# Fifteen constant matmuls into an unread PSUM tile ahead of each attention layer

## The chip, the cores and the metric

The kernel runs on one core of one Trainium2 chip. The metric is the device time of one execution in microseconds, the median over several runs. The core has a matmul engine (TensorE, in the profile PE, its weight loads PEld), a vector engine (VectorE, DVE), an activation engine (ScalarE, ACT), GpSimd (POOL) and a queue for transfers (SyncE, SP). Matmuls write to PSUM, which has eight banks; the other engines copy the results from there to SBUF.

## The reference

Four layers run one after the other on an array `x` of 2048 positions by 512 channels: convolution, attention, convolution, attention. Each adds its result to `x`, and each works on a layer norm of `x`. The two convolutions share their parameters, and so do the two attention layers.

```python
x = A_u
x = x + _A_ref(_layernorm(x), ...)            # long convolution, as a product of spectra
x = x + _B_ref(_layernorm(x), B_wqkv, B_wo)   # attention over 8 positions, 2 apart
x = x + _A_ref(_layernorm(x), ...)
x = x + _B_ref(_layernorm(x), B_wqkv, B_wo)

def _B_ref(x, wqkv, wo):                      # H = 32 heads of 16, W = 8, dil = 2
    q, k, v = split(x @ wqkv)
    logits = einsum("bhsd,bhswd->bhsw", q, k[pos - 2*w]) * 16 ** -0.5   # w = 0..7, masked before 0
    o = einsum("bhsw,bhswd->bhsd", softmax(logits), v[pos - 2*w])
    return o.reshape(B, S, D) @ wo
```

## The kernel before, in words

`x` stays in SBUF as a tile `X` of 128 partitions by 16 groups `j` by 512 channels. `kernel_and_first_conv` builds the convolution's kernel and does the first convolution; `b_layer` does an attention layer; `a_layer` does the second convolution; `b_layer` is then called again. In what follows, the first place is the passage from the first convolution to the first attention layer, and the second place is the passage from the second convolution to the second attention layer.

Inside a layer the order of the work on each engine is fixed: the layer records its operations in a `Plan`, and `Plan.run` issues them in the order of a written list of numbers. What an engine has in its queue is done in that order. Semaphores hold an instruction until its operands are ready and until the PSUM or SBUF buffer that it writes has been read by its last user. PSUM pools are opened per layer, so the first tile of a pool in `b_layer` lies in banks that the convolution before it used.

A convolution ends with the matmuls into `ps_y` (L849 and L852 in the first one, L1089 and L1092 in the second), which ScalarE copies back to `X` (L856 and L1097).

An attention layer begins with its layer norm. For each of four groups of four `j`, VectorE gathers the statistics of `X` (L150, L159), ScalarE takes the root (L163), VectorE inverts it and makes the offset (L175, L187), and the two engines write the normed rows `xn` (VectorE at L190, ScalarE at L1154). Two of the eight pairs of rows are transposed by TensorE, eight 128x128 matmuls each, into `pt_x` (L1165), and copied to `xnT` by ScalarE (L1168). The other six pairs are transposed by transfers (L1160). From `xnT` TensorE makes the values `ps_v` (L1210, eight matmuls of 256 columns for a pair) and the queries and keys `ps_qk` (L1190, four matmuls of 512 columns for each block), which ScalarE and VectorE copy to `VX`, `qT` and `kT` (L1215, L1195). `ps_v` and `ps_qk` take turns in a pool `psA` of two PSUM banks. VectorE then multiplies `qT` with shifted `kT` into `prod` (L1241), TensorE sums these into `Lp` (L1251), and after the softmax VectorE multiplies the weights with shifted `VX` (L1353), TensorE sums over `w` (L1369, L1374) and multiplies with `wo` (L1426).

`ident` is the 128x128 identity and `C["F1T"]` a constant table of the convolution; both are loaded once at the start and stay in SBUF.

Of the kernel before, what the change touches and what calls it, by code (L numbers as in the profile page):

```python
# [13 lines left out]
F32 = mybir.dt.float32  # L14
# [1104 lines left out]
def b_layer(nc, tc, C, X, Wt, VX, ln_b, part, evac, done, VSTAT_Q):  # L1119

    with ExitStack() as es:
# [8 lines left out]
        psA = es.enter_context(tc.tile_pool(name="b_psA", bufs=2, space=PSUM))  # L1130
        ident, bones = C["ident"], C["bones"]
# [3 lines left out]
        kT = [qk.tile([128, 2, NK * 128 + S], BF, name=f"kT{fp}") for fp in range(2)]  # L1135
        qT = [qk.tile([128, 2, S], BF, name=f"qT{fp}") for fp in range(2)]
        L = [sm.tile([128, NJ, 2, W, 8], BF, name=f"L{fp}") for fp in range(2)]
        box = {}
        pl = Plan(psA=2, psL=1, psO=2, prod=4, LT=3, sm1=1, sm2=1, sm_m=1, sm_s=1, rdb=1)
        turned, Kd, Qd, Kx, Vd, Ld, Sd, Od = {}, {}, {}, {}, {}, {}, {}, {}  # L1140
# [88 lines left out]
        def logits(fp, jh, halves):  # L1229
# [46 lines left out]
            def evac():  # L1276
                nc.scalar.copy(L[fp][:, j0:j0 + 8].rearrange("p j t (q w) h -> p q (j t) (w h)", q=2),
                               box.pop(("l", fp, jh))[:].rearrange("p q b j (t x) -> p q (b j t) x", t=2))
# [11 lines left out]
        def softmax(fp, j0, j1):  # L1290
            n = j1 - j0
            Lf = L[fp][:, j0:j1].rearrange("p j t w h -> p (j t) w h")

# [19 lines left out]
            def mask():  # L1313
                for w in range(1, W):
                    k = min(j1, DIL * w)
                    if k > j0:
                        nc.gpsimd.memset(L[fp][0:1, j0:k, :, w, :], -1e9)

# [26 lines left out]
        def pv(fp, j0, nj):  # L1345
            flat, np = fp == 0 or j0 < 12, min(nj, 4)

            def part(w, first):
                a = j0 - DIL * w

                def prod():
# [3 lines left out]
                        VX[:, fp, NV + a:NV + a + nj].rearrange("p j (t d h) -> p (j t) d h", t=2, d=DH),  # L1355
                        L[fp][:, j0:j0 + nj, :, w, :].rearrange("p j t h -> p (j t) h").unsqueeze(2)
                        .to_broadcast([128, nj * 2, DH, 8]), ALU.mult)
# [120 lines left out]
def kernel(  # L1478
# [36 lines left out]
    with tc.manual_schedule():  # L1515
        with tc.tile_pool(name="mid", bufs=1) as mid:
# [40 lines left out]
            def stored(pl, q, after):  # L1557
                pl.op("S", 2.0, lambda: nc.sync.dma_start(ov[:, q * 4:q * 4 + 4, :], X[:, q * 4:q * 4 + 4, :]), *after, lag=2.7)
            b_layer(nc, tc, C, X, Wt, VX, ln_b, 2, summed, normed, BN_Q)
            a_layer(nc, tc, C, X, kt_dram, U, ln_b2)  # L1560
        b_layer(nc, tc, C, X, Wt, VX, ln_b2, 1, lambda j, ps: nc.scalar.copy(X[:, j, :], ps), stored, range(4))


# [28 lines left out]
```

## Time and profile before

| | |
|---|---|
| median of 6 runs | 530.82 us (530.10 to 531.24) |
| the profiled execution's own time | 530.8 us |
| its span, first to last instruction | 528.9 us |
| mean granted TensorE clock | 0.962 |
| PE busy | 406.0 us, 77% of the span |
| DVE busy | 475.5 us, 90% |
| ACT busy | 339.3 us, 64% |

Busy time is the time in which an engine has at least one instruction running; matmuls overlap, so a busy PE is not PE at its peak. The granted clock is a record of its own: 1.00 is full speed, 0.50 half. In a table by windows, each row is a stretch of the span in us from its start, with each engine's busy time and count of instructions, the granted clock and the transfers. In the chain of work that ended last, each row has its start, its length and what ran.

### The profile page before, as it was taken

To read this page: it belongs to the slowest core of one execution; us is meant where nothing else is said; L and a number is where in the kernel's file an instruction comes from. 1 tells how busy PE (TensorE), PEld (TensorE's weight loads), DVE (VectorE), ACT (ScalarE), POOL (GpSimd) and SP (SyncE) were. 2 spreads that over 40 slices of the span, in tenths; PEclk is the share of its full clock that TensorE was granted. 3 is DMA by queue.
4 is the path that set the end of the run, shared out by engine and by line. 5 is a ranking of instruction groups with operands and counts; after the bars stand their busy time and mean duration, and the time that the engine had idled before them with its cause. 6 is when DMAs were issued, how large, how long until landed. Compare 5 with 4: busy or idle time off the path is not lost.

```text
span 528.9 us, 11869 instructions
## 1 busy us (share of the span) xinstructions
PE 406.0 (77%) x4943; PEld 239.5 (45%) x4943; DVE 475.5 (90%) x803; ACT 339.3 (64%) x505; POOL 12.9 (2%) x62
## 2 busy tenths in 40 slices
PE   0202367689868769689999779969994999997896
PEld 0100244456655547443356334555773433652352
DVE  4999999999999999749899998889989497999995
ACT  3999956886856758662666137989996436641230
POOL 0000000000000003000000000000000000000000
PEclk9999997989988989979999999999997999998998
DMA  8300074248135253460011522679401500232242
GB/s 265 152 1 0 0 141 93 59 127 149 43 122 102 61 142 101 144 120 31 0 56 46 100 50 40 152 234 174 81 2 20 101 30 32 71 50 60 40 131 89
DMA packets 88922, 45.08 MB, mean 85 GB/s; under 512 B 74923, under 2 KB 81068, under 8 KB 88612
## 3 DMA queue, kind: packets, MB, share of 16 engines
q1 hardware_dynamic: 87284, 43.93, 34.7%
q8 instruction: 38, 0.62, 0.5%
q10 hardware_dynamic: 1584, 0.39, 0.4%
q14 instruction: 16, 0.13, 0.1%
HBM read 15.77 MB, written 8.13 MB: 45 GB/s over the span
## 4 chain that ended last, share of the span: by engine, by line
PE 37%; DVE 31%; ACT 10%; issue 8%; DMA 3%; POOL 0%; SPq 0%; DVEq 0%; ACTq 0%
PE ps_qk L1190 11%; DVE prod L1353 6%; PE ps_v L1210 4%; PE Lp L1251 3%; DVE Ttab L488 3%; DVE Ttab L481 3%; DVE ln_st_b L150 2%; DVE Y2tab L545 2%; DVE Ttab L545 2%; DVE Ttab L480 2%; PE po L1369 2%; PE ps_o L1426 2%; PE po L1374 1%; ACT X L598 1%; DVE prod L1241 1%
## 5 line engine op out<-in xcount | busy, mean ns | idle before, releaser
L1241 DVE TENSOR_TENSOR prod<-qT,kT 128x2048 bf16<-128x2048 bf16 (+1 forms) x80 | 77.1, 1004 | 15.0 <-ACT kT L1195 14.3
L1353 DVE TENSOR_TENSOR prod<-VX,L 128x2048 bf16<-128x2048 bf16 (+2 forms) x96 | 77.5, 861 | 1.9 <-PE po L1374 0.9
L1190 PE MATMUL ps_qk<-xnT,wqk 128*128 128x512 bf16 x256 | 63.1, 385 | 0.1
L1369 PE MATMUL po<-prod,sb_ident 128*128 128x512 bf16 x224 | 56.0, 386 | 7.3 <-DVE prod L1353 4.9
L1369 PEld LDWEIGHTS <-sb_ident 128*128 128x128 bf16 x224 | 21.7, 99 | 35.8 <-issue 12.3
L1190 PEld LDWEIGHTS <-wqk 128*128 128x128 bf16 x256 | 22.6, 99 | 31.6 <-issue 10.8
L1210 PE MATMUL ps_v<-wv,xnT 128*128 128x256 bf16 x256 | 34.4, 281 | 0.8 <-ACT xnT L1168 0.6
L1389 ACT CAST ot<-po 128x1024 bf16<-128x1024 f32 x14 | 13.6, 1014 | 30.0 <-PE po L1369 30.0
L1251 PE MATMUL Lp<-prod,sb_bones 128*32 128x512 bf16 x256 | 28.6, 388 | 4.2 <-DVE prod L1241 4.2
L520 PE MATMUL ps_sum<-Ttab,sb_ident 128*128 128x512 bf16 x18 | 7.8, 433 | 30.4 <-DVE Ttab L480 27.6
L716 ACT CAST Z<-ps_s 128x1024 bf16<-128x1024 f32 (+1 forms) x32 | 29.3, 988 | 0.8 <-PE ps_s L711 0.4
L1215 ACT CAST VX<-ps_v 128x512 bf16<-128x512 f32 x32 | 18.8, 587 | 17.0 <-PE ps_v L1210 17.0
L558 PE MATMUL psk<-Ttab 128*32 128x64 bf16 x1024 | 21.8, 205 | 9.6 <-DVE Ttab L545 6.1
L545 DVE TENSOR_TENSOR Ttab<-Ttab,MPA 128x2048 bf16<-128x2048 bf16 (+2 forms) x20 | 28.4, 1433 | 0.3
L1210 PEld LDWEIGHTS <-xnT 128*128 128x128 bf16 x256 | 23.9, 100 | 9.8 <-issue 4.6
L1426 PE MATMUL ps_o<-wo_t,oT 128*128 128x512 bf16 x112 | 28.0, 379 | 0.0
L561 PE MATMUL psk<-Y2tab,Ttab 128*32 128x48 bf16 x1024 | 21.9, 200 | 7.1 <-issue 7.1
L545 DVE TENSOR_TENSOR Y2tab<-Ttab,MPB 128x6144 bf16<-128x6144 bf16 (+1 forms) x13 | 27.2, 2118 | 0.0
L150 DVE BATCH_NORM_STATS2 ln_st_b<-X 128x6 f32<-128x128 bf16 (+2 forms) x80 | 23.0, 357 | 3.7 <-ACT X L856 3.3
L1195 ACT CAST kT<-ps_qk 128x512 bf16<-128x512 f32 x26 | 15.2, 584 | 16.8 <-PE ps_qk L1190 16.8
L1195 ACT CAST qT<-ps_qk 128x512 bf16<-128x512 f32 x24 | 14.0, 584 | 18.5 <-PE ps_qk L1190 18.5
L558 PEld LDWEIGHTS <-Ttab 128*32 128x32 bf16 x1024 | 19.8, 103 | 12.2 <-issue 11.5
(218 smaller groups left out, 1024.8 us busy)
## 6 DMA issues: line engine op xcount, KB each, us to landing
X<-in_A_u_dram SPq DMA_DIRECT2D x8, 512.0 KB, 5.3
kt_scratch<-sp_k SPq DMA_DIRECT2D x16, 256.0 KB, 3.1
Kt<-kt_scratch SPq DMA_DIRECT2D x16, 256.0 KB, 6.1
out_dram<-X SPq DMA_DIRECT2D x4, 512.0 KB, 2.7
k_scratch<-KTq SPq DMA_DIRECT2D x7, 256.0 KB, 2.7
KT<-k_scratch SPq DMA_DIRECT2D x7, 256.0 KB, 3.0
VX<-VX SPq DMA_DIRECT2D x4, 448.0 KB, 3.8
kT<-kT SPq DMA_DIRECT2D x8, 192.0 KB, 2.2
```

The source lines that it names most:

```text
L150: self.nc.vector.bn_stats(self.st[:, j, part, :], X[:, j, a:b])
L545: nc.vector.tensor_tensor(d, src.to_broadcast([128, c, n, 2 * EYB]), mm.to_broadcast([128, c * n, EYB, 2]), ALU.mult)
L558: nc.tensor.matmul(o.rearrange("e (s i) -> e s i", s=2), xs, T[:, 1:3, h, m // 2, :, t], start=(m == 0), stop=False, skip_group_check=True)
L716: nc.scalar.copy(box["Z", kind, dc][:, 0:n // 8, :, jq * 32:(jq + 1) * 32].rearrange("p g r k -> p r g k"), box.pop(("s1", kind, dc, jq))[ ...
L1190: nc.tensor.matmul(ps[:], wqk[:, ct, f0:f0 + 128], xnT[:, 4 * s:4 * s + 4, ct, :], start=(ct == 0), stop=(ct == 3))
L1195: copy((qT, kT)[which][fp][:, f2, o:o + 512], box.pop(("qk", which, fp, f2, s))[:])
L1210: nc.tensor.matmul(ps[:, jj].rearrange("p t h d -> p (t h d)"), xnT[:, j + jj, ct, :], wv[:, ct, fp * 256:(fp + 1) * 256], start=(ct == 0) ...
L1241: nc.vector.tensor_tensor(pr[:, 0:n2], qT[fp][:, a:a + n2, j0 * 128:j0 * 128 + 1024], kT[fp][:, a:a + n2, c0:c0 + 1024], ALU.mult)
L1251: nc.tensor.matmul(Lp[r0:r0 + 32, w // 4, :], bones[:, w % 4, :], pr[:, f2 - a, hb * 512:(hb + 1) * 512], start=(n == 1), stop=(n == 4), s ...
L1353: nc.vector.tensor_tensor(p2[:, 0:nj].rearrange("p j t d h -> p (j t) d h"), VX[:, fp, NV + a:NV + a + nj].rearrange("p j (t d h) -> p (j ...
L1369: nc.tensor.matmul(po[:, c:c + 512], ident[:], p2[:, k + j:k + j + 2].rearrange("p j t d h -> p (j t d h)"), start=(n == 1), stop=(n == W))
L1426: nc.tensor.matmul(ps, box["oT"][:, ft // 2, j, ft % 2, :], wo_t[:, ft, :], start=(ft == 0 and not res), stop=(ft == 3))
```

## The change

Right after `b_layer` has made its tiles and before it records its plan, it takes a tile `idle` of one PSUM bank from `psA` and issues fifteen matmuls of 128 rows by 512 columns into it. The weights are `ident`, the moving operand is the first two groups of `F1T`. Each starts and ends its own sum, so each overwrites the one before. Nothing reads the tile. As `b_layer` is called twice, thirty matmuls and thirty loads of `ident` are added in all.

```diff
         L = [sm.tile([128, NJ, 2, W, 8], BF, name=f"L{fp}") for fp in range(2)]
+        idle = psA.tile([128, 512], F32, name="idle", tag="psA")
+        for _ in range(15):
+            nc.tensor.matmul(idle[:], ident[:], C["F1T"][:, 0:2].rearrange("p j r k -> p (j r k)"), start=True, stop=True)
         box = {}
         pl = Plan(psA=2, psL=1, psO=2, prod=4, LT=3, sm1=1, sm2=1, sm_m=1, sm_s=1, rdb=1)
```

In TensorE's queue the fifteen stand behind the last `ps_y` matmul of the convolution and ahead of the first `pt_x` transpose. The first of them waits for ScalarE: for the copy of the last `ps_y` tile to `X`. The first user of `psA` in the plan, a `ps_v`, moves from the pool's first bank to its second, and all later users move along with it. The queues of the other engines are the same as before.

## The prediction

> **What bounds the kernel now.** The page gives two limits that take turns:
>
> ```profile
> PE 406.0 (77%) x4943; PEld 239.5 (45%) x4943; DVE 475.5 (90%) x803; ACT 339.3 (64%) x505; POOL 12.9 (2%) x62
> ...
> PE 37%; DVE 31%; ACT 10%; issue 8%; DMA 3%; POOL 0%; SPq 0%; DVEq 0%; ACTq 0%
> ```
>
> The first line is busy time, the second the shares of the chain that ended last. PE leads the chain although DVE is busier, so there are stages in which PE alone sets the end. The chain in order of time shows one of them at the first place:
>
> ```profile
> 225.59 0.82 ACT xn L1154
> 226.41 0.05 issue
> 226.46 1.05 PE pt_x L1165 x8
> ...
> 227.58 1.02 ACT xnT L1168
> 228.60 0.05 issue
> 228.65 1.89 PE ps_v L1210 x8
> 230.54 8.71 PE ps_qk L1190 x36
> ```
>
> and at the second:
>
> ```profile
> 406.26 1.05 PE pt_x L1165 x8
> ...
> 408.45 1.69 PE ps_v L1210 x8
> 410.14 7.77 PE ps_qk L1190 x36
> ```
>
> The same 36 matmuls take 8.71 us at one place and 7.77 at the other, and the 8 into `ps_v` 1.89 and 1.69, where later in the layer the chain has them at 0.98. What differs is the clock. I then asked for windows of 3.41 us, the step in which the clock record changes in this trace:
>
> ```profile
> 222.08:225.50 3.42, 0.00 (x0) 0.00 (x0) 3.42 (x29) 1.22 (x4) 0.00 (x0) 1.00 0.00 0
> 225.50:228.91 3.41, 2.15 (x18) 1.82 (x19) 3.41 (x13) 2.92 (x5) 0.00 (x0) 0.50 0.13 25
> 228.91:232.32 3.41, 3.41 (x13) 1.74 (x12) 1.23 (x4) 1.22 (x3) 0.00 (x0) 0.50 1.05 192
> 232.32:235.74 3.42, 3.42 (x17) 1.57 (x16) 0.00 (x0) 2.30 (x4) 0.00 (x0) 1.00 1.12 189
> 399.58:402.99 3.41, 0.52 (x9) 0.35 (x7) 3.41 (x17) 1.37 (x3) 0.00 (x0) 1.00 0.00 0
> 402.99:406.40 3.41, 0.14 (x2) 0.15 (x3) 3.41 (x28) 2.19 (x5) 0.00 (x0) 0.50 0.00 0
> 406.40:409.82 3.42, 3.11 (x23) 2.48 (x22) 3.42 (x14) 1.93 (x2) 0.00 (x0) 0.50 0.40 75
> ...
> 146.99:150.40 3.41, 1.44 (x12) 0.82 (x12) 3.41 (x6) 3.41 (x4) 0.00 (x0) 1.00 0.53 196
> 177.71:181.12 3.41, 1.46 (x173) 1.34 (x159) 3.41 (x7) 2.31 (x3) 0.00 (x0) 1.00 0.13 27
> ...
> 474.67:478.08 3.41, 1.39 (x12) 0.58 (x8) 3.19 (x4) 0.55 (x2) 0.00 (x0) 1.00 1.12 128
> ```
>
> The first figure after the length is PE busy, the third from the end the granted clock. A window in which PE rested (0.00 and 0.52 us) is followed by windows at half clock. At the first place the clock is half from 225.50 to 232.32, at the second from 402.99 to 409.82. PE restarts at 226.46 and 406.26, so 5.86 us and 3.56 us of half clock fall on work. The last three rows place the border: 1.44 us (42%) and 1.39 us (41%) closed the clock for the next window, 1.46 us (43%) did not. For opening, the window with 2.15 us (63%) at 225.50 did not do it, the one with 3.11 us (91%) at 406.40 did. The rest comes from layer norm: PE's two waits for `xn` are 4.74 and 6.15 us.
>
> **Does earlier PE work move the end?** At the first place DVE has nothing to do from 230.14 to 238.18 but wait for `kT`, which comes from the `ps_qk` blocks. From 240 to 325 it is over 90% busy in nearly every stretch. So DVE starts earlier by what PE wins, and the rest of the layer with it. The transfers could spoil this: six transposes by transfer are issued from 227.26 to 234.10 and land at most 4.0 us later, so by 238.1 at the latest. The block that reads the last of them starts at 241.66, and 2.3 us earlier is 239.4, still behind the landing. The blocks that read the first two start at about 235.2, or 232.9 with the gain, against landings by 228.63 + 4.0 = 232.6. This cover is thin (0.3 us); typical landings at 3.4 us leave 0.9.
>
> **The burst itself.** A 512-column matmul at full clock takes its turn every 0.216 us (7.77 / 36), and the loads of `ident` hide under it: the chain has 8 of the `po` matmuls, which also load `ident` each time, in 1.73 us, 0.216 each. Fifteen take 3.24 us. At the first place they wait for the last copy L856, which ends at 221.92 + 0.57 = 222.49; the burst issues from about 222.55 to 225.79 and the first transpose wants PE at 226.46, so 0.67 us are spare. At the second place the last copy L1097 ends at about 400.73, the burst goes from 400.8 to 404.0, and 2.2 us are spare. The windows before both bursts are 76% and over 90% busy, so both start at full clock. The burst is therefore free as long as one matmul takes under (226.46 - 222.55) / 15 = 0.26 us. Nothing but the transposes stands behind the waiting instruction on PE, and they wait longer for `xn`. The change of bank in `psA` costs nothing: both banks are free long before the first `ps_v`.
>
> **First place, gain.** With the burst, the window at 222.08 is some 85% busy. The one at 225.50 has 0.45 us of burst, two groups of transposes at about 0.6 us each and 0.7 us of `ps_v`, together 2.3 us or 69%. Both are above 43%, the clock stays full. Then:
> the first 8 transposes, 1.05 us at half clock, take 0.61, the row of 8 matmuls of the same shape into `ps_y` at full clock: 0.44 won. ACT's copy keeps its 1.02. The 8 `ps_v` go from 1.89 to 0.98: 0.91. The 36 `ps_qk` go from 8.71 to 7.77: 0.94. Sum 2.29 us.
>
> **Second place, gain.** All at full clock it is 0.44 + (1.69 - 0.98) = 1.15 us. But after the burst PE rests 2.2 us. With windows at the same instants, the one from 402.99 to 406.40 holds the burst up to its last end near 404.18, 1.19 us, and 0.14 us of transposes: 1.33 us or 39%, just under the border. Then the clock closes at 406.40 instead of 402.99, opens at 409.82 as before, and almost nothing is won. The windows are not tied to the program's start as far as one trace can say. A window starting between about 402.6 and 405.0, 2.4 of 3.41 us, would close the clock; the others would not. I take 30% of 1.15, 0.35 us, with 0 and 1.15 as ends. It is nearer the lower end because the 39% row is.
>
> **Two rules of the Trainium skill.** The page "TensorE: Matmul & The Clock Gate" says in its closing table ("Why this matters for your kernels") that only gaps of PE above about 3 us are to be feared. By that rule the second place, with 2.2 us left, would win its full 1.15, and the sum below would be 3.4; the 39% against the 41% and 42% that closed the clock here makes me keep 0.35.
> The same page says in "Part 4: PE-mode transpose" that transposes do not count as busy for the clock gate. This speaks against the change: without the transposes the window at 225.50 would fall to about 1.1 us, 33%, and the clock would close at 228.91 for one window on work that PE bounds, which gives back up to 1.7 us. The trace does not settle it, since the window with 63% that failed to open was mostly transposes.
>
> **Sum.** By the profiled execution 2.29 + 0.35 = 2.6 us. Other executions will meet the windows elsewhere. If the clock before had opened one window earlier at the first place (228.91), only 0.44 and a little of `ps_v` would have been lost there, some 0.6 us; so its loss lies between 0.6 and 2.3, and I estimate 1.6 as its mean, with a slightly larger gain of 0.5 at the second place: 2.1. Between 2.1 and 2.6 I take 2.3. The profiled execution's own time, 530.8, is the median's, 530.82, so the forecast is 530.8 - 2.3 = 528.5 us.
>
> **The rivals.**
> *The gate closes behind the burst at the first place as well* (because transposes count little, or the border is higher than 43%). Half clock from 228.91 to 232.32 costs about 1.7 of the 2.29; 0.6 us remain, and nothing at the second place: 530.2. For it: the window with 63% that failed to open held mostly transposes, and so would this one. Against: 69% is far above the 43% that kept the clock open. Here too belongs the case that the earlier start is eaten by the thin cover of the transfers. Chance 0.14.
> *Slower: the closed clock is moved from rest onto work, for two windows.* Today part of the half clock falls on PE's rest. If the gate closes behind the burst at both places and needs two windows to open, as it did at 225.50, 6.83 us of half clock lie wholly on PE's path and cost 3.41 us at each place, against 2.29 and 1.15 now: 530.8 + 6.8 - 3.4 = 534.2. It decides if the first window after closing is under some 63 to 91% busy. Against it: behind the transposes PE is busy without a break (3.41 of 3.41 us at 228.91). Chance 0.10; the smaller forms of it between 531.9 and 534.2 are in that.
> *The forecast*, with at least the first place won: 0.76, between 527.3 (2.29 + 1.15) and 529.7.
>
> A measurement of this kernel can tell about 0.2%, 1.06 us, from no change: the six times spread over 1.14 us. Faster by more needs over 1.06 us: 0.76. The first rival lies within: 0.14. Slower: 0.10. The range for 8 in 10 goes from 527.2, both places won, to 530.4, which takes in the first rival's price and leaves out the slower one.
>
> **What would show it.** In the profile after: no half clock between 222 and 240; `pt_x` x8 near 0.6 us, `ps_v` x8 near 1.0, the 36 `ps_qk` near 7.8; the burst ending before `xn`, with PE's wait for `xn` at the first place down from 4.74 to about 0.7 us, at the second from 6.15 to about 2.2; DVE's first `prod` 2.3 us earlier after the restart. A clock of 0.50 right behind 228 would be the first rival; two such windows at both places the slower one. A first transpose that waits for the burst would make the burst's price wrong; an unmoved `prod` behind a faster `ps_qk` would make the path wrong.

## The result and the profile after

The changed kernel takes 527.43 us (median of 21 runs, 526.07 to 530.73), the kernel before, run beside it, 530.39 us (44 runs, 528.86 to 532.13). The ratio is 0.995, with an interval at 95% of 0.994 to 0.9961: 2.65 us faster by the ratio, 2.96 by the medians. The forecast was 528.5 us, the range 527.2 to 530.4, and faster had 0.76 of the chance. The profiled execution took 526.27 us and its span is 524.4 us; in its mean the granted clock rose from 0.962 to 0.981. It is one of the fastest executions of the changed kernel, so its stretches show more than the median has.

Line numbers behind the change are three higher than before: `pt_x` is L1168, `ps_v` L1213, `ps_qk` L1193, `Lp` L1254. The timeline of PE at the two places, with start, length, what ran, and in brackets the idle time before it and what ended it:

```profile
221.31 3.40 PE L1140 MATMUL idle<-sb_F1T,sb_ident 128*128 128x512 bf16 x15 [0.81 <-ACT X L856]
225.24 1.33 PE L1168 MATMUL pt_x<-sb_ident,xn 128*128 128x128 bf16 x16 [0.54 <-ACT xn L1157]
227.02 1.05 PE L1213 MATMUL ps_v<-wv,xnT 128*128 128x256 bf16 x8 [0.45 <-ACT xnT L1171]
227.93 7.93 PE L1193 MATMUL ps_qk<-xnT,wqk 128*128 128x512 bf16 x36
235.79 0.39 PE L1254 MATMUL Lp<-prod,sb_bones 128*32 128x512 bf16 x2
...
397.39 3.40 PE L1140 MATMUL idle<-sb_F1T,sb_ident 128*128 128x512 bf16 x15 [0.67 <-ACT X L1097]
402.87 1.07 PE L1168 MATMUL pt_x<-sb_ident,xn 128*128 128x128 bf16 x16 [2.08 <-ACT xn L1157]
404.65 1.05 PE L1213 MATMUL ps_v<-wv,xnT 128*128 128x256 bf16 x8 [0.71 <-ACT xnT L1171]
...
410.20 3.61 PE L1193 MATMUL ps_qk<-xnT,wqk 128*128 128x512 bf16 x16 [0.16 <-DMA xnT<-xn]
413.75 0.39 PE L1254 MATMUL Lp<-prod,sb_bones 128*32 128x512 bf16 x2
```

The burst fills the rest at the first place but for 0.54 us; at the second 2.08 us are left. `ps_v` takes 1.05 us at both places, where it took 1.89 and 1.69. (The profile has not every matmul on record: bursts of 15 and 25 appear as x14 or x15 and x24.) The windows of 3.41 us at this execution's own clock steps (PE busy is the first figure after the length, the granted clock the third from the end):

```profile
221.12:224.54 3.42, 3.23 (x15) 1.36 (x14) 3.42 (x29) 1.20 (x5) 0.00 (x0) 1.00 0.00 0
224.54:227.95 3.41, 2.34 (x26) 1.72 (x26) 3.41 (x14) 3.28 (x4) 0.00 (x0) 1.00 0.22 42
...
398.62:402.04 3.42, 2.17 (x11) 0.78 (x8) 3.42 (x29) 1.52 (x5) 0.00 (x0) 1.00 0.00 0
402.04:405.45 3.41, 1.86 (x24) 1.62 (x25) 3.40 (x18) 2.83 (x5) 0.00 (x0) 1.00 0.09 18
```

PE is busy for 95% and 69% of the two windows at the first place, 64% and 55% at the second, and the clock is 1.00 throughout.

Cut at the first transpose and the first `Lp` matmul of each place, the two profiled executions compare like this:

| stretch | before, us | after, us | difference |
|---|---|---|---|
| start to the first transpose of the first place | 226.46 | 225.24 | -1.22 |
| from there to the first `Lp` matmul | 12.72 | 10.55 | -2.17 |
| to the first transpose of the second place | 167.08 | 167.08 | 0.00 |
| from there to the first `Lp` matmul | 11.59 | 10.87 | -0.72 |
| to the end | 111.01 | 110.69 | -0.32 |

The second and fourth rows are the change. What is won there is not given back: the 167 us between the places are the same to 0.01. (In two of the profiles below they aren't: with one matmul they are 168.29 us, with a stretch of half clock at 310.33 us.) The difference in the first row lies ahead of the burst: from the last `ps_y` matmul to the first transpose it is 4.96 us in both. So the burst can't have made it. The last row isn't the burst's either: all ten changed kernels have 110.67 to 110.70 us there, the one with nothing added at the second place too, and in the profile of before the stretch has a transfer (`VX<-VX`, 5.16 us in its chain) that VectorE waited for. Over the profiles of all kernels told of here (30 matmuls at the first place left aside) the first transpose of the first place comes between 225.15 and 226.46 us. This is a reason to judge the change by medians and by stretches, and not by two spans.

### The profile page after: what moved, and what is told of

It reads as the page before. It is cut to its first block, busy times and chain, and to the rows that moved or that the text cites. A ratio compares the mean times of both kernels' runs of the same rounds, so it can differ in the third digit from the quotient of the medians.

```text
span 524.4 us, 11929 instructions
## 1 busy us (share of the span) xinstructions
PE 407.0 (78%) x4973; PEld 238.5 (45%) x4973; DVE 475.3 (91%) x803; ACT 339.1 (65%) x505; POOL 12.9 (2%) x62
## 4 chain that ended last, share of the span: by engine, by line
DVE 34%; PE 31%; ACT 9%; issue 8%; DMA 6%; SPq 1%; POOL 0%; DVEq 0%; ACTq 0%
PE ps_qk L1193 10%; DVE prod L1356 7%; PE ps_v L1213 4%; PE Lp L1254 3%; DVE Y2tab L545 3%; DVE Ttab L545 3%; DVE Ttab L488 3%; DVE ln_st_b L150 3%; DVE Ttab L481 3%; DVE Ttab L480 3%; DMA Kt<-kt_scratch 2%; PE po L1372 2%; DVE pb L803 1%; ACT X L598 1%; DVE Ttab L497 1%
## 5 line engine op out<-in xcount | busy, mean ns | idle before, releaser
L1193 PE MATMUL ps_qk<-xnT,wqk 128*128 128x512 bf16 x256 | 62.3, 380 | 0.3 <-DMA xnT<-xn 0.2
L1193 PEld LDWEIGHTS <-wqk 128*128 128x128 bf16 x256 | 22.2, 98 | 31.2 <-issue 10.1
L1213 PE MATMUL ps_v<-wv,xnT 128*128 128x256 bf16 x256 | 32.9, 273 | 1.4 <-ACT xnT L1171 1.2
L1254 PE MATMUL Lp<-prod,sb_bones 128*32 128x512 bf16 x256 | 28.7, 388 | 4.2 <-DVE prod L1244 4.2
L1213 PEld LDWEIGHTS <-xnT 128*128 128x128 bf16 x256 | 23.3, 98 | 9.6 <-issue 4.6
L830 ACT CAST VT<-vp 128x512 bf16<-128x512 f32 x31 | 16.9, 597 | 11.9 <-PE vp L826 11.0
```

The costliest lines, as they stand in the source:

```text
L1193: nc.tensor.matmul(ps[:], wqk[:, ct, f0:f0 + 128], xnT[:, 4 * s:4 * s + 4, ct, :], start=(ct == 0), stop=(ct == 3))
L1213: nc.tensor.matmul(ps[:, jj].rearrange("p t h d -> p (t h d)"), xnT[:, j + jj, ct, :], wv[:, ct, fp * 256:(fp + 1) * 256], start=(ct == 0) ...
L1254: nc.tensor.matmul(Lp[r0:r0 + 32, w // 4, :], bones[:, w % 4, :], pr[:, f2 - a, hb * 512:(hb + 1) * 512], start=(n == 1), stop=(n == 4), s ...
```

## The experiments

The last two columns of this table are the time from the first transpose to the first `Lp` matmul at each place, in that kernel's profile. The kernel before was run beside each group: 530.47, 530.27 and, for the last row, 530.33 us.

| matmuls at the first, second place | median, us | ratio to before (95%) | first | second |
|---|---|---|---|---|
| none (before) | 530.39 | | 12.72 | 11.59 |
| 15, 15 (changed) | 527.43 | 0.995 (0.994 to 0.9961) | 10.55 | 10.87 |
| 15, 0 | 528.19 | 0.9959 (0.9942 to 0.9975) | 10.55 | 11.94 |
| 0, 15 | 529.24 | 0.9972 (0.9956 to 0.9987) | 13.02 | 11.55 |
| 1, 1 | 529.68 | 0.9986 (0.9977 to 0.9994) | 11.44 | 12.02 |
| 15, 25 | 526.26 | 0.9923 (0.9909 to 0.9938) | 10.55 | 10.55 |
| 60, 100 transposes | 526.59 | 0.9937 (0.9922 to 0.9951) | 10.55 | 10.66 |
| 60, 100 of 128 columns | 527.12 | 0.9945 (0.993 to 0.9959) | 10.55 | 10.82 |
| 30, 25 | 529.20 | 0.9988 (0.9976 to 1.0) | 10.54 | 10.55 |
| 8, 25 | 527.22 | 0.9945 (0.9928 to 0.9962) | 11.93 | 10.77 |
| 1, 1 again | 529.68 | 0.9988 (0.9975 to 1.0001) | 12.96 | 11.70 |

My theory: the burst keeps TensorE's clock from being halved while layer norm leaves it without work, and each place is worth the half clock it saves. The rivals: the gain comes from something else that the edit brought (the wait, the turned banks); and, for the size, transposes or short rests count otherwise than I took them to.

**One place at a time.** `b_layer` is called with `part` 2 for the first attention layer and 1 for the second.

```diff
+        if part == 2:    # second kernel: part == 1
-        idle = psA.tile(...)
+            idle = psA.tile(...)
...
```

> The fifteen matmuls at the first place alone. If the clock is what the burst buys, and buys it place by place: from the first transpose to the first Lp matmul 10.6 us at the first place, as in the changed kernel, and 11.0 to 12.7 at the second, as in the kernel before; 2.0 us under the kernel before. Rival, that the gain comes from something that both places share (the turn of the banks in psA, the layout of the program): the gain is either halved, 1.5 us, or gone, and the first place is not at 10.6.

> The fifteen matmuls at the second place alone. Clock theory: the first place keeps 11.7 to 12.7 us from the first transpose to the first Lp matmul; the second place has 10.6 to 10.9 where the window grid leaves the clock open and 11.6 or more where it closes behind the burst; 0.4 to 0.9 us under the kernel before, within what can just be told. Rival, both places worth the same: 1.5 us.

The first place alone won 2.28 us by the medians, with 10.55 us at the place that has the burst and 11.94 at the one without. The second place alone won 1.23 us, more than the 0.4 to 0.9 expected, though the profiled execution won nothing there (11.55). Its windows say why:

```profile
399.99:403.40 3.41, 2.68 (x16) 1.28 (x14) 3.41 (x20) 1.07 (x3) 0.00 (x0) 1.00 0.00 0
403.40:406.82 3.42, 1.33 (x13) 0.65 (x11) 3.41 (x26) 2.19 (x5) 0.00 (x0) 1.00 0.00 0
406.82:410.23 3.41, 3.10 (x21) 2.15 (x18) 3.41 (x13) 2.03 (x3) 0.00 (x0) 0.50 0.47 89
```

The rest of 2.09 us behind the burst leaves a window 39% busy, and the next one has half clock. That is the row worked out ahead for the second place (1.33 us, 39%). The twelve times of this kernel run from 527.49 to 530.54 us, six below 529.0 and six above 529.5. Two groups like that are what a clock that stays open in some executions and closes in others would leave; the profile caught one of the latter. The clocks fit: the granted clock over a whole execution is 0.968 to 0.975 in the six below 529.0 and 0.962 to 0.969 in the others.

**One matmul.** The tile, the wait and the turned banks without the burst:

```diff
-        for _ in range(15):
+        for _ in range(1):
```

> One matmul in place of fifteen, at both places: the tile, the wait for the last copy of X and the turned banks stay, the burst goes. Clock theory: the same time as the kernel before within 0.3 us, and half clock at both places from before the first transpose on. Rival, that the wait or the banks made the gain: 2.5 to 3 us under the kernel before.

> One matmul at both places once more, unchanged, since the first run of it came out 0.14% under the kernel before (interval 0.05% to 0.23%) where nothing was expected. If that was chance of where the windows fell: within 0.15% of the kernel before on either side, interval taking in 1. If the tile, the wait or the banks are worth something of their own: again 0.1% to 0.2% under it, 0.5 to 1.0 us.

In the first of the two profiles the windows at the two places are:

```profile
221.58:224.99 3.41, 0.02 (x1) 0.00 (x0) 3.41 (x27) 1.57 (x4) 0.00 (x0) 1.00 0.00 0
224.99:228.40 3.41, 2.94 (x22) 2.37 (x23) 3.41 (x11) 2.74 (x4) 0.00 (x0) 0.50 0.39 73
...
399.07:402.49 3.42, 0.38 (x1) 0.00 (x0) 3.42 (x23) 0.87 (x3) 0.00 (x0) 1.00 0.00 0
402.49:405.90 3.41, 1.02 (x10) 1.03 (x11) 3.40 (x24) 1.90 (x4) 0.00 (x0) 0.50 0.00 0
405.90:409.31 3.41, 3.10 (x19) 2.07 (x17) 3.32 (x12) 2.24 (x3) 0.00 (x0) 0.50 0.66 125
```

The burst is what matters: with one matmul, both places have half clock again and 11.44 to 12.96 us. But the time was 0.79 and 0.65 us under the kernel before, 529.68 us both times. The first interval leaves 1 out, the second takes it in. The two profiles are ahead of the one of before from the start to the first transpose (225.15 and 225.45 us against 226.46), which is ahead of the change, and in the last stretch, as all the others are. No stretch of the traces shows a gain that belongs to the single matmul, so this remainder of some 0.7 us stays open. If it is real, it is part of the changed kernel's gain too.

**A burst that reaches the transposes.** Fifteen at the first place, twenty-five at the second:

```diff
-        for _ in range(15):
+        for _ in range(15 if part == 2 else 25):
```

> Fifteen at the first place and twenty-five at the second, which fills 5.4 of its 6.15 us of rest: 397.4 + 5.4 = 402.8 against the first transpose at 402.87 in the changed kernel. Clock theory: no window near the second place falls under 43%, so the clock is full there in each execution; the median is 0.3 to 0.8 us under the changed kernel's and the times spread less upwards. Rival, that 15 already keep the clock there (gaps under 3 us are harmless): the same as the changed kernel. Second rival: the last of the burst delays the first transpose, 0.1 to 0.3 us slower than the changed kernel.

It is the fastest kernel of this study: 526.26 us, 1.17 under the changed one by the medians and more than the 0.3 to 0.8 expected, with times from 525.78 to 527.51. The interval of its ratio ends just under where that of the changed kernel begins. At the second place PE has no rest left ahead of the transposes:

```profile
397.49 5.56 PE L1140 MATMUL idle<-sb_F1T,sb_ident 128*128 128x512 bf16 x24 [0.67 <-ACT X L1097]
402.97 1.07 PE L1168 MATMUL pt_x<-sb_ident,xn 128*128 128x128 bf16 x16
```

From the last `ps_y` matmul to the first transpose it takes 6.38 us, as before the change (406.26 - 399.88), so the first transpose isn't delayed, and the place is at 10.55 us.

**Transposes.** Do they count as work for the clock? The same time filled with transposes, and as a control with plain matmuls of the same shape:

```diff
-        idle = psA.tile([128, 512], F32, name="idle", tag="psA")
-        for _ in range(15):
-            nc.tensor.matmul(idle[:], ident[:], ...)
+        idle = psA.tile([128, 8, 128], BF, name="idle", tag="psA")
+        for k in range(60 if part == 2 else 100):
+            nc.tensor.transpose(idle[:, k % 8, :], C["F1T"][:, 0, 0, :], ident[:])

         # control, with idle as [128, 4, 128] in F32:
+            nc.tensor.matmul(idle[:, k % 4, :], C["F1T"][:, 0, 0, :], ident[:], start=True, stop=True)
```

> Transposes of 128 columns in place of the matmuls of 512, over the same time: 60 at the first place and 100 at the second, each with the same constant as weights and the identity moving, compared with the kernel of 15 and 25 matmuls (526.3 us). If transposes count as work for the clock: full clock at both places, 10.55 us from the first transpose to the first Lp matmul, 526 to 527 us. If they don't: half clock behind the burst or already inside it, 11.4 to 13 us at both places, 529 to 531 us; where the clock closes inside the burst, the burst also ends late and the time is up to 2 us more.

> The control to the run before: the same 60 and 100 instructions of 128 columns, with the same operands, as plain matmuls. If it is the time on the array that counts: as with 15 and 25 matmuls of 512 columns, 526 to 527 us, 10.55 us at both places. If the many loads of weights or the narrow shape count against it: as with transposes.

They do count for keeping the clock open. With transposes only, the windows are:

```profile
221.34:224.75 3.41, 3.33 (x60) 3.32 (x59) 3.41 (x29) 1.19 (x5) 0.00 (x0) 1.00 0.00 0
224.75:228.17 3.42, 2.46 (x29) 1.80 (x27) 3.42 (x13) 3.18 (x4) 0.00 (x0) 1.00 0.25 48
398.82:402.24 3.42, 3.42 (x65) 3.42 (x63) 3.42 (x30) 1.61 (x5) 0.00 (x0) 1.00 0.00 0
402.24:405.65 3.41, 2.70 (x42) 2.45 (x40) 3.40 (x17) 2.75 (x4) 0.00 (x0) 1.00 0.12 23
```

The third holds nothing but transposes, and the clock behind it is full. The page "TensorE: Matmul & The Clock Gate" of the Trainium skill says in "Part 4: PE-mode transpose" that a transpose doesn't count as busy the same way as a matmul does. These rows disagree, at least for holding the clock and if this kernel's transposes run in the mode that the page means: the profile lists them as MATMUL, and a hundred take 5.74 us, as the plain matmuls of the control do. Whether transposes alone would open a closed clock wasn't tried. The control came out the same within the intervals.

**Too many, too few.**

```diff
-        for _ in range(15):
+        for _ in range(30 if part == 2 else 25):    # second kernel: 8 instead of 30
```

> Thirty matmuls at the first place, twenty-five at the second. The burst then takes 6.5 us where 3.9 are free: the first transpose comes 2.5 us late, with PE's wait for xn gone, and the time is 2.2 to 2.6 us above the kernel of 15 and 25, 528.5 to 529. Rival, that DVE or the transfers have slack there and take the delay up: under 1 us.

> Eight matmuls at the first place, twenty-five at the second: 1.73 us of burst, then 2.2 us of rest, as the changed kernel has it at the second place. If the share of work in a window decides: half clock behind the rest in about two of three executions, 0.5 to 2 us above the kernel of 15 and 25 in the median (526.8 to 528.3), with a wide spread from 526 to 528.5. If only a rest of over about 3 us closes the clock: no difference, 526.3 in all.

Thirty at the first place move the burst onto the path, as its chain of waits shows:

```profile
222.37 6.20 PE idle L1140 x28
228.58 0.46 PE pt_x L1168 x8
229.04 0.02 issue
```

From the last `ps_y` to the first transpose it is 7.50 us, against 4.96 with fifteen: 2.54 more, and the median is 2.94 above the kernel of 15 and 25. Nothing behind it takes the delay up; nearly all of the gain is gone (529.20).

Eight leave 2.04 us of rest at the first place. In the profile this window had 38% and the next one half clock:

```profile
223.45:226.87 3.42, 1.29 (x17) 0.90 (x16) 3.42 (x20) 2.37 (x4) 0.00 (x0) 1.00 0.00 0
226.87:230.28 3.41, 2.96 (x13) 1.64 (x12) 2.41 (x8) 1.96 (x3) 0.00 (x0) 0.50 0.81 151
```

The place took 11.93 us instead of 10.55, and the four times are 526.23, 526.57, 527.87 and 528.02: 0.96 us above the kernel of 15 and 25 in the median. The granted clock is 0.978 in the two faster ones and 0.972 and 0.973 in the others. So a rest of 2 us can be enough to close the clock, and the share of work in a window is what fits. The skill's rule to have no gaps above about 3 us (same page, "Why this matters for your kernels") is not enough in this kernel.

## Why the prediction was right

**The burst.** Worked out at 0.216 us a matmul and 3.24 us in all, free at both places, with 0.67 and 2.2 us to spare: PE's wait for `xn` behind it is 0.54 and 2.08 us, and the first copy to wait for is the one named. The kernel with thirty shows the point from which it costs.

**The first place.** 2.29 us forecast, 2.17 measured in the stretch, 2.28 with that place alone. The terms: `ps_v` won 0.84 by the timeline (1.89 to 1.05) against 0.91, and the first `prod` of VectorE starts 9.55 us behind the first transpose, not 11.72. The 0.44 for the transposes was won in that ACT could start its first copy right behind its second `xn`; the transposes left the chain there. The 69% for the window behind the burst is what the profile has (2.34 of 3.41). That is in part luck: this window happens to begin 0.70 us ahead of the first transpose, where the sum took the 0.96 us of the profile before.

**The second place.** The two ends, 0 and 1.15, are both real: 11.55 us with the clock closed behind the burst, 10.55 with it open all the way, against 11.59 before. The rule that I kept against the skill's, a border in the busy share and not in the length of the rest, held at both places: 38 and 39% closed the clock, 55% and more did not. But 41 to 43% was read too sharply. The profile before has a busier window that closed it, which the prediction doesn't show:

```profile
160.64:164.06 3.42, 1.51 (x19) 1.14 (x20) 3.42 (x7) 3.16 (x4) 0.00 (x0) 1.00 0.87 209
164.06:167.48 3.42, 3.42 (x17) 2.21 (x16) 3.42 (x7) 0.28 (x1) 0.00 (x0) 0.50 1.24 159
```

That is 44%, more than the 43% that kept the clock open. The weight of the second place may have been sized too low: 0.35, or 0.5 as a mean over executions, where the place alone won 1.23 us (1.5 by the ratio, with 0.7 to 2.3 as its interval). The remainder of one matmul may be in this 1.23. The profiles without a burst at the second place have 11.59, 11.94, 12.02 and 11.70 us there, 1.26 above 10.55 on average, so there is a little more to win than in the one execution that I read.

**The mean over executions.** The forecast is 1.07 us above the result. Of this 0.43 us is that the kernel before has 530.39 us over more runs and not 530.82. Of the rest, 0.64 us, some 0.3 comes from shading: the unshaded sum was 2.6, the forecast took 2.3. The four profiles without a burst at the first place have 12.72, 13.02, 11.44 and 12.96 us, 2.0 above 10.55 on average: the case in which the clock opens one window earlier occurs (11.44), but it costs 0.9 us and not 0.6, and was one in four. The unshaded 2.6 is nearer the measured 2.65 to 2.96.

There is another reading. The two places alone won 2.28 and 1.23 us, 3.51 together, more than both at once. If each of these gains has the remainder of some 0.7 us in it, the places are worth some 1.6 and 0.5 us, the prediction's own means, and what it left out is the remainder. Against the kernel with one matmul (529.68) the changed one is 2.25 us faster; the forecast was 2.3. The runs don't decide between the two readings. Nor do they show why three of the 21 executions of the changed kernel took 529.66 to 530.73 us, as long as the kernel before. (The lower end that goes with the chance of 0.76 should read 527.4 by its own terms, not 527.3.)

**The thin cover.** The transfers that feed the `ps_qk` blocks were named as the first thing to run short. At the first place they did not. At the second PE waited 0.16 us for one, and its stretch is 10.87 and not 10.55 us with the clock at full speed. The transfers there landed up to 4.3 us behind their issue; the sum for the first place had 4.0 as the longest.

**The rivals.** The first one, a clock that closes behind the burst at the first place, did not come in the three profiles with fifteen matmuls there; it came with eight. The slower one needed two closed windows behind the burst; where the clock closed behind a burst (0 and 15; 8 and 25), one window opened it again.

## What to carry to other kernels

Look at the granted clock where an engine's work resumes after a rest, not at its mean over the span: here 5.86 and 3.56 us of half clock on a path that PE bounds cost 2.2 and 1.0 us, while the mean was 0.96. Constant matmuls in the rest are free as long as they end before the next operand comes, and they have to reach nearly to it: 2 us of rest behind them are enough to lose part of the gain in some executions, and 2.5 us too many lose it nearly all. Judge such a change by stretches and medians, since where the clock's windows fall differs from execution to execution.

## What the runs showed of the hardware

- In each profile the clock changes at multiples of 3.413 us from one another, but their distance from the start of the span differs: modulo 3.413 it is 0.22, 2.68, 1.61, 0.63 and 3.13 us in the profiles of the first five rows of the table of experiments. The windows are not tied to the program.
- In all eleven profiles every window of full clock in which PE was busy for less than 42% was followed by half clock, and none of 46% or more was. Between these both occur: 45% closed it (one matmul again, 153.28 to 156.69), 42% did not (15 and 15, 74.36 to 77.77). Opening takes more: a window of 86% (one matmul, 224.99 to 228.40) opened it, one of 80% (burst at the second place alone, 225.91 to 229.32, first place) did not. Here too there is no sharp border: one of 78% opened it (before, 150.40 to 153.82).
- This holds from the first change on record, 66 to 69 us into each profile. Ahead of it the windows print 1.00, but the profile before has matmuls of 512 columns at 0.58 to 0.63 us there (48.42 to 50.37), as long as at half clock (0.63 at 230.33) and not 0.38 as at full. So that 1.00 is not a measured clock, and the mean over the span is too high.
- Transposes hold the clock open like matmuls: 60 in 3.5 us and 100 in 5.7 us.
